# Threshold attention in front of a routed expert layer: the attention rewritten as a five-step pipeline with a written order on every engine

## The chip, the cores and the metric

The kernel runs on one core of one Trainium2 chip. The time is the device time of one execution in microseconds (us); the median of three runs stands for the kernel. A core has five engines that run their own instruction streams and wait for each other through semaphores: TensorE (PE, with its weight loads as PEld), VectorE (DVE), ScalarE (ACT), GpSimd (POOL) and SyncE (SP, which here issues DMAs). TensorE writes to PSUM only; POOL can't reach PSUM.

## The reference

Attention over 8 batches, 8 heads, 576 rows and 64 columns, with a threshold below the row's maximum, then a two-layer expert network whose expert follows from the token's id:

```python
scores = (1 / sqrt(64)) * (q @ k.transpose(0, 1, 3, 2))          # (8, 8, 576, 576)
thresh = scores.max(-1, keepdims=True) - tau
scores = where(scores >= thresh, scores, -1e9)
attn = exp(scores - scores.max(-1, keepdims=True))
attn = attn / (attn.sum(-1, keepdims=True) + 1e-09)
x = (attn @ v).transpose(0, 2, 1, 3).reshape(4608, 512)
expert = token_ids * 2654435761 % 8
for e in range(8):
    out[expert == e] = maximum(x[expert == e] @ w1[e], 0) @ w2[e]  # 512 -> 1024 -> 512
```

All of it is fp32.

## The kernel before

Two heads are worked on together, a pair `p`; there are 32 of them. k and q come in transposed, the 64 columns of one head on partitions 0 to 63 and those of the other on 64 to 127, so that the score matmuls of the two heads use the two row halves of TensorE's array. A pair has nine score tiles of 128 rows and 576 columns: four for each head (units 0 to 7) and one (unit 8) that holds the last 64 rows of both heads. A tile takes two PSUM banks, and `ps_sc` has room for two tiles.

`score` (L135) issues the matmuls of two tiles and calls `weigh` (L156) for each: the row maximum from PSUM on DVE (L160), two operations on one column each that make the exponent's bias and the threshold (L161, L163), the exponential from PSUM on ACT (L167), and on DVE the mask (L169): it compares the scores, read from PSUM a second time, with the threshold, multiplies with the exponentials and sums the row. `turn_head` and `turn_tail` (L174, L188) transpose the masked weights `w` of a pair in pieces of 128 by 128, four to a PSUM bank, and ACT copies each bank to `wT` in SBUF (L186, L194, L199). `av_half` (L202) multiplies them with v, 288 columns at a time, the two heads in the two column halves of the array. `put_x` (L218) copies the result to `oT`, transposes it back, scales it by the row sums (DVE, L243, L247) into a tile for the whole batch, and after every fourth pair `store_x` (L253) writes the batch to `x_scratch` in HBM from POOL's queue.

`route` (L262) builds the table that tells which tokens each expert gets. It is called once, after the second pair's scores. The main loop (L422 on) writes out the order of TensorE's instructions by hand: in round `p` the five groups of scores of pair `p` alternate with the transposes, AV and output of pair `p - 1`. The order on the other engines is the scheduler's. The experts' part (L448 on) follows: it gathers rows of x by the table (POOL), transposes them, and runs two chains of matmuls for each expert (L479, L493).

## Time and profile before

| | before |
|---|---|
| time, median of 3 runs | 1472.01 us (1471.65 to 1475.71) |
| profiled execution: time, span | 1471.82 us, 1470.2 us |
| busy share of the span: PE, PEld, DVE, ACT, POOL | 85%, 51%, 43%, 33%, 8% |
| mean granted TensorE clock | 0.955 |
| DMA, mean over the span | 62 GB/s |
| chain of work that ended last | "issue" 8%, DMA 2%: it is only followed through the last stores |

The shares are means over two parts with different limits: up to about 880 us DVE and ACT work all the time and PE has gaps; behind that PE is full and the others are nearly idle. So the profile is read by stretches of time, and within attention by the waits of each engine. The page's chain that ended last covers the last 147 us alone and says nothing about attention.

### The profile page before, as it was taken

What the parts mean: (1) busy time and instruction counts of PE and PEld (TensorE: products, weight loads), DVE (VectorE), ACT (ScalarE), POOL (GpSimd) and SP (SyncE); (2) the same over time, 40 slices, a digit from 0 to 9 for tenths busy, and PEclk for the clock granted to TensorE, in tenths of its full rate; (3) what the DMA queues carried; (4) which work ended last, traced back from release to release, by engine and by line L of the source; (5) the groups of instructions that cost most, each with busy time, mean ns of one, the idle gap of its engine ahead of it and who ended that gap; (6) DMA issues with size and microseconds to landing.
All of it is one profiled execution on the core that took longest, in us unless ns stands there. A gap on an engine that the chain in (4) does not pass through costs nothing. (4 is left out here: it accounts for less than half of the span.)

```text
span 1470.2 us, 15795 instructions
## 1 busy us (share of the span) xinstructions
PE 1249.7 (85%) x5894; PEld 746.4 (51%) x5894; DVE 633.1 (43%) x1773; ACT 483.9 (33%) x809; POOL 111.7 (8%) x127
## 2 busy tenths in 40 slices
PE   4568777878878787887878777999999999999997
PEld 2344445544544554445544445565656564646463
DVE  5756676666666666676666651101000101001000
ACT  2334545455454554545455540000000000000000
POOL 0030000000000000000000004101010202010101
PEclk9878999999899999999899998999999999999999
DMA  8200210210201102012001003223232313121000
GB/s 304 70 8 26 81 33 17 88 26 23 91 17 56 58 24 91 17 33 81 25 26 49 1 18 114 95 85 107 74 108 69 110 69 118 62 86 59 32 1 33
DMA packets 41198, 91.27 MB, mean 62 GB/s; under 512 B 9116, under 2 KB 9116, under 8 KB 41120
## 3 DMA queue, kind: packets, MB, share of 16 engines
q1 hardware_dynamic: 32032, 61.91, 13.0%
q0 software_dynamic: 9088, 28.32, 5.7%
q8 instruction: 48, 0.79, 0.2%
q14 instruction: 30, 0.25, 0.1%
HBM read 72.39 MB, written 19.92 MB: 63 GB/s over the span
## 5 line engine op out<-in xcount | busy, mean ns | idle before, releaser
L151 PE MATMUL sc<-k_sb,q 64*128 64x288 f32 (+1 forms) x1152 | 259.4, 460 | 88.5 <-DVE w L169 69.3
L167 ACT ACTIVATE w<-sc,bia,scl 128x576 f32<-128x576 f32 x288 | 225.9, 830 | 194.6 <-DVE bia L161 194.5
L184 PE MATMUL tr<-ident,w 128*128 128x128 f32 (+1 forms) x1280 | 209.7, 312 | 86.0 <-ACT wT L186 84.3
L160 DVE TENSOR_REDUCE mx<-sc 128x1 f32<-128x576 f32 x288 | 207.1, 753 | 174.5 <-PE sc L151 174.3
L493 PE MATMUL o_ps<-w_sb,h_sb 128*128 128x512 f32 x640 | 280.6, 592 | 0.0
L479 PE MATMUL h_ps<-xT,w_sb 128*128 128x320 f32 x1024 | 277.5, 433 | 0.0
L169 DVE SCALAR_TENSOR_TENSOR w<-sc,thr,w 128x576 f32<-128x576 f32 x288 | 225.3, 816 | 102.4 <-ACT w L167 101.4
L186 ACT COPY wT<-tr 128x512 f32<-128x512 f32 (+1 forms) x320 | 176.6, 591 | 193.1 <-PE tr L184 192.9
L479 PEld LDWEIGHTS h_ps<-xT,w_sb 128*128 128x128 f32 x1024 | 194.9, 190 | 83.4 <-issue 3.7
L151 PEld LDWEIGHTS sc<-k_sb,q 64*128 64x128 f32 (+1 forms) x1152 | 138.7, 198 | 184.1 <-issue 121.2
L184 PEld LDWEIGHTS tr<-ident,w 128*128 128x128 f32 (+1 forms) x1280 | 154.0, 151 | 152.5 <-ACT wT L186 117.8
L493 PEld LDWEIGHTS o_ps<-w_sb,h_sb 128*128 128x128 f32 x640 | 118.9, 190 | 136.0 <-issue 135.8
L213 PE MATMUL av<-wT,v_sb 128*64 128x288 f32 (+1 forms) x1280 | 178.7, 415 | 0.0
L487 DVE TENSOR_SCALAR h_sb<-h_ps 128x640 f32<-128x640 f32 x32 | 26.4, 825 | 298.9 <-PE h_ps L479 288.4
L213 PEld LDWEIGHTS av<-wT,v_sb 128*64 128x64 f32 (+1 forms) x1280 | 80.3, 135 | 84.6 <-issue 46.5
L496 ACT COPY o_sb<-o_ps 128x512 f32<-128x512 f32 x40 | 23.4, 586 | 300.5 <-PE o_ps L493 300.5
L472 DVE COPY xT<-xT_ps 128x512 f32<-128x512 f32 x40 | 27.6, 690 | 193.3 <-PE xT_ps L471 192.3
L485 ACT ACTIVATE h_sb<-h_ps 128x640 f32<-128x640 f32 x32 | 22.5, 704 | 239.3 <-PE h_ps L479 239.3
L260 POOL DMA_DIRECT2D x_scratch<-xt x16 | 9.9, 619 | 776.6 <-DVE xt L247 776.6
L463 POOL DMA_INDIRECT xg<-x_scratch,gidx x40 | 40.6, 1016 | 273.4 <-PE xT_ps L471 264.0
L161 DVE TENSOR_SCALAR bia<-mx,nscl 128x1 f32<-128x1 f32 x288 | 58.7, 204 | 0.0
L163 DVE TENSOR_SCALAR thr<-mx,drop 128x1 f32<-128x1 f32 x288 | 58.7, 204 | 0.0
(92 smaller groups left out, 380.6 us busy)
## 6 DMA issues: line engine op xcount, KB each, us to landing
w_sb<-in_moe_w_dram SPq DMA_DIRECT2D x16, 2048.0 KB, 8.8
k_sb<-in_k_dram SPq DMA_DIRECT2D x32, 288.0 KB, 2.9
q<-in_q_dram SPq DMA_DIRECT2D x32, 256.0 KB, 2.7
v_sb<-in_v_dram SPq DMA_DIRECT2D x8, 1024.0 KB, 5.4
x_scratch<-xm POOLq DMA_DIRECT2D x8, 1024.0 KB
q<-in_q_dram SPq DMA_DIRECT2D x64, 16.0 KB, 2.6
v_sb<-in_v_dram SPq DMA_DIRECT2D x8, 128.0 KB, 4.0
x_scratch<-xt POOLq DMA_DIRECT2D x16, 64.0 KB
```

The costliest lines, as they stand in the source:

```text
L151: nc.tensor.matmul(scs[u][:, i, 0:S2], lhsT=q_sb[rows, cols], rhs=k_sb[rows, S2 * i:S2 * i + S2], start=True, stop=True)
L160: nc.vector.tensor_reduce(out=mx[:], in_=sc[:, :, 0:S2], axis=AX.XY, op=ALU.max)
L161: nc.vector.tensor_scalar(out=bia[:], in0=mx[:], scalar1=nscl[:], scalar2=None, op0=ALU.mult)
L163: nc.vector.tensor_scalar(out=thr[:], in0=mx[:], scalar1=drop[:], scalar2=None, op0=ALU.subtract)
L167: nc.scalar.activation(w3, sc[:, :, 0:S2], AF.Exp, bias=bia[:], scale=scl[:])
L169: nc.vector.scalar_tensor_tensor(out=w3, in0=sc[:, :, 0:S2], scalar=thr[:], in1=w3, op0=ALU.is_ge, op1=ALU.mult, accum_out=rs[:, u:u + 1])
L184: nc.tensor.transpose(tr[0:kn, P * t:P * t + P], ws[4 * j + t][:, k0:k0 + kn], ident[:])
L186: nc.scalar.copy(wT[0:kn, c, j, 0:TAIL], tr[0:kn, :])
L213: nc.tensor.matmul(av[64 * j:64 * j + 64, i, 0:S2], lhsT=v_sb[0:kn, c, h * D:h * D + D], rhs=wT[0:kn, c, j, S2 * i:S2 * i + S2], start=(c ...
L463: nc.gpsimd.indirect_dma_start(out=xg[:], out_offset=None, in_=x_dram[:, :], in_offset=bass.IndirectOffsetOnAxis(ap=idx, axis=0), bounds_c ...
L479: nc.tensor.matmul(h_ps[:, i, 0:width], lhsT=w1_sb[:, co, fo * P:fo * P + P], rhs=xT[:, co, i * width:i * width + width], start=(co == 0), ...
L493: nc.tensor.matmul(o_ps[:], lhsT=h_sb[:, fo, kt * P:kt * P + P], rhs=w2_sb[:, fo, :], start=(fo == 0), stop=(fo == FO - 1))
```

## The change

Attention becomes a pipeline over 160 steps `n`, five for each pair (`p, s = divmod(n, 5)`; in step s = 0 the tile with the last rows of both heads, in s = 1 to 4 one tile of each head). In step `n` the engines do:

- scores of step `n + 1` (PE), into the same two PSUM tiles;
- `negate` of step `n` (DVE): one operation copies a tile from PSUM to SBUF as `ns`, with the sign changed, and gives the row minimum of that; POOL adds the threshold (`thr`); ACT takes the exponential from `ns`;
- `mask` of step `n - 1` (DVE), from `ns` and `w`, both in SBUF;
- `turn_w` and `put_wT` of step `n - 2`: transposes by halves of 64 rows into the two banks of one PSUM tile, and one copy of 640 columns by ACT;
- AV of the pair before, in four parts over s = 1 to 4 (320 columns in s = 1 and 2, 256 in s = 3 and 4), `put_oT` behind each half;
- in s = 0 the output of the pair two back: `turn_o` writes its transposes into the PSUM tile of AV, `put_x` scales them (one DVE operation, two on ACT) and SP stores x for that pair.

The factor 1/8 and the case of a negative tau go into q (`scale_q`, on POOL). v is loaded per pair. The last chunk of `w` and v is filled up with zeros to 128. `route` is a generator, one piece of which is issued behind each step from `n = 7` on. The order is written out for all engines, not for TensorE alone. The ten zeroed buffers of the expert part are set up by POOL at the start instead of by DVE behind attention; the first experts' weights are loaded from pair 20 on instead of pair 4.

TensorE's order for one pair. Before, from the third score group of a pair to the next pair's first; `sc` are scores, `tr` with `w` turned weights, `tr` with `oT` the output turned back:

```order
L151 MATMUL sc<-k_sb,q_117 128x288 x4
L184 MATMUL tr<-ident,w 128x128 x16
L184 MATMUL tr<-ident,w 64x128 x4
L151 MATMUL sc<-k_sb,q_117 128x288 x4
L193 MATMUL tr<-ident,w 128x128 x4
L198 MATMUL tr<-ident,w 64x128
L213 MATMUL av<-wT,v_sb 64x288 x10
L151 MATMUL sc<-k_sb,q_117 128x288 x4
L213 MATMUL av<-wT,v_sb 64x288 x10
L151 MATMUL sc<-k_sb,q_117 128x288 x2
L238 MATMUL tr<-ident,oT 128x128 x4
```

Now, from step s = 1 of a pair to its step s = 4:

```order
L241 MATMUL av<-wT_a,v_121 64x320 x4
L215 MATMUL tr<-ident,w_124 128x64 x10
L168 MATMUL sc<-k_sb,q_119 128x288 x4
L215 MATMUL tr<-ident,w_125 128x64 x10
L241 MATMUL av<-wT_a,v_121 64x320 x6
L215 MATMUL tr<-ident,w_126 128x64 x10
L168 MATMUL sc<-k_sb,q_119 128x288 x4
L241 MATMUL av<-wT_b,v_121 64x256 x6
L215 MATMUL tr<-ident,w_127 128x64 x10
L168 MATMUL sc<-k_sb,q_119 128x288 x4
L215 MATMUL tr<-ident,w_128 128x64 x10
```

AV stands in four parts of two or three chunks instead of two of five, and a turned tile is ten short transposes in one row instead of a share of sixteen and four.

DVE's order, before, two groups of scores:

```order
L160 TENSOR_REDUCE mx<-sc 128x1 x2
L161 TENSOR_SCALAR bia<-mx,nscl 128x1
L163 TENSOR_SCALAR thr<-mx,drop 128x1
L161 TENSOR_SCALAR bia<-mx,nscl 128x1
L163 TENSOR_SCALAR thr<-mx,drop 128x1
L169 SCALAR_TENSOR_TENSOR w,rs<-sc,thr,w 128x576 x2
L160 TENSOR_REDUCE mx<-sc 128x1 x2
```

Now, from step s = 3 to the output scaling in the next pair's s = 0:

```order
L180 TENSOR_SCALAR ns,nmx<-sc 128x576 x2
L204 SCALAR_TENSOR_TENSOR w_126,rs<-ns,thr,w_126 128x576
L204 SCALAR_TENSOR_TENSOR w_127,rs<-ns,thr,w_127 128x576
L180 TENSOR_SCALAR ns,nmx<-sc 128x576 x2
L204 SCALAR_TENSOR_TENSOR w_128,rs<-ns,thr,w_128 128x576
L204 SCALAR_TENSOR_TENSOR w_129,rs<-ns,thr,w_129 128x576
L180 TENSOR_SCALAR ns,nmx<-sc 128x576
L204 SCALAR_TENSOR_TENSOR w_123,rs<-ns,thr,w_123 128x576
L204 SCALAR_TENSOR_TENSOR w_124,rs<-ns,thr,w_124 128x576
L256 TENSOR_SCALAR rec<-rs 128x9
L258 RECIPROCAL rec<-rec 128x9
```

The first two-tile operation of a step frees the scores' PSUM tiles, and the masks that follow are those of the step before.

The diff, cut to its core (of the lines taken out, most of which are printed above, only some stand here):

```diff
+    WA, WB = 64 + 2 * P, 2 * P
...
+         tc.tile_pool(name="a_ns", bufs=5) as a_ns, \
...
-         tc.tile_pool(name="ps_tr", bufs=2, space=PSUM) as ps_tr, \
+         tc.tile_pool(name="ps_tr", bufs=1, space=PSUM) as ps_tr, \
...
+        v_bufs = [a_q.tile([P, NC, P], FP32, name=f"v_{i}") for i in range(3)]
+        NW = 7
+        w_bufs = [a_q.tile([P, NC * P], FP32, name=f"w_{i}") for i in range(NW)]
+        wT = [a_q.tile([P, 2, NC, WA], FP32, name="wT_a"),
+              a_q.tile([P, 2, NC, WB], FP32, name="wT_b")]
+        oT = a_o.tile([P, 64 + S], FP32, name="oT")
+        av = ps_av.tile([P, 2, 512], FP32, name="av")
...
+            for j in range(2):
+                nc.sync.dma_start(out=q_sb[64 * j:64 * j + 64, TAIL + 64 * j:TAIL + 64 * j + 64],
+                                  in_=qT[b, h0 + j, :, TAIL:S])
             nc.sync.dma_start(out=k_sb[:], in_=kT[b, h0:h0 + 2].rearrange("h d s -> (h d) s"))
...
+        def load_v(p):
+            b, hp = divmod(p, HP)
+            v_sb = v_bufs[p % 3]
+            rows = v[b].rearrange("s h d -> s (h d)")[:, hp * P:hp * P + P]
+            nc.sync.dma_start(out=v_sb[:, 0:4],
+                              in_=rows[0:TAIL].rearrange("(c p) m -> p c m", p=P))
+            nc.sync.dma_start(out=v_sb[0:64, 4], in_=rows[TAIL:S])
+        def scale_q(p):
+            q_sb = q_bufs[p % 3]
+            nc.gpsimd.tensor_scalar(out=q_sb[:], in0=q_sb[:], scalar1=keep_any[:], scalar2=SCALE,
+                                    op0=ALU.mult, op1=ALU.mult)
+        def heads(n):
+            return 1 if n % NS == 0 else 2
+        def score(n):
+            p, s = divmod(n, NS)
             q_sb, k_sb = q_bufs[p % 3], kts[p]
-            scs = {}
-            for u in us:
-                sc_new = ps_sc.tile([P, 2, 512], FP32, name="sc")
-                scs[u] = sc_new
+            for j in range(heads(n)):
+                sc = ps_sc.tile([P, 2, 512], FP32, name="sc")
+                scs[n, j] = sc
             for i in range(2):
-                for u in us:
...
+                for j in range(heads(n)):
+                    if s == 0:
+                        rows, cols = slice(0, P), slice(TAIL, TAIL + P)
                     else:
-                        rows, cols = slice(0, P), slice(TAIL, TAIL + P)
-                    nc.tensor.matmul(scs[u][:, i, 0:S2], lhsT=q_sb[rows, cols],
+                        rows, cols = slice(64 * j, 64 * j + 64), slice(P * (s - 1), P * s)
+                    nc.tensor.matmul(scs[n, j][:, i, 0:S2], lhsT=q_sb[rows, cols],
...
-                weigh(p, u, scs[u])
...
-            w = a_w.tile([P, S], FP32, name="w")
-            w3 = w[:].rearrange("p (i s) -> p i s", i=2)
-            nc.scalar.activation(w3, sc[:, :, 0:S2], AF.Exp, bias=bia[:], scale=scl[:])
-            rs = pend[p]["rs"]
-            nc.vector.scalar_tensor_tensor(out=w3, in0=sc[:, :, 0:S2], scalar=thr[:], in1=w3,
-                                           op0=ALU.is_ge, op1=ALU.mult,
-                                           accum_out=rs[:, u:u + 1])
-            pend[p]["w"][u] = w
...
-                    nc.tensor.transpose(tr[0:kn, P * t:P * t + P],
-                                        ws[4 * j + t][:, k0:k0 + kn], ident[:])
-                nc.scalar.copy(wT[0:kn, c, j, 0:TAIL], tr[0:kn, :])
...
+        def negate(n):
+            nmx = a_st.tile([P, 2], FP32, name="nmx")
...
+            stats[n] = (nmx, thr)
+            for j in range(heads(n)):
+                sc = scs.pop((n, j))
+                ns = a_ns.tile([P, S], FP32, name="ns")
+                nss[n, j] = ns
+                nc.vector.tensor_scalar(out=ns[:].rearrange("p (i s) -> p i s", i=2),
+                                        in0=sc[:, :, 0:S2], scalar1=-1.0, scalar2=None,
+                                        op0=ALU.mult, op1=ALU.min, accum_out=nmx[:, j:j + 1])
+            nj = heads(n)
+            nc.gpsimd.tensor_scalar(out=thr[:, 0:nj], in0=nmx[:, 0:nj], scalar1=drop[:],
+                                    scalar2=None, op0=ALU.add)
+        def expo(n, j):
+            w = w_bufs[w_count[0] % NW]
...
+            ws[n, j] = w
+            nc.scalar.activation(w[:, 0:S], nss[n, j][:], AF.Exp, bias=stats[n][0][:, j:j + 1],
+                                 scale=-1.0)
...
+        def mask(n, j):
...
+            u = 8 if s == 0 else 2 * (s - 1) + j
+            w = ws[n, j]
+            nc.vector.scalar_tensor_tensor(out=w[:, 0:S], in0=nss.pop((n, j))[:],
+                                           scalar=stats[n][1][:, j:j + 1], in1=w[:, 0:S],
+                                           op0=ALU.is_le, op1=ALU.mult,
+                                           accum_out=rss[p][:, u:u + 1])
+        def turn(dst, src, cols):
+            for c, (lo, hi) in enumerate(cols):
+                for r, c0 in ((0, lo), (1, hi)):
+                    rows = slice(64 * r, 64 * r + 64)
+                    nc.tensor.transpose(dst[:, r, 64 * c:64 * c + 64], src[rows, c0:c0 + P],
+                                        ident[rows, rows])
+        KCOLS = [(P * c, P * c) for c in range(NC)]
+        def turn_w(n, j):
+            tr = ps_tr.tile([P, 2, 512], FP32, name="tr")
+            turn(tr, ws.pop((n, j)), KCOLS)
+            return tr
+        def put_wT(n, j, tr):
+            s = n % NS
+            src = tr[:, :, 0:64 * NC].rearrange("p r (c q) -> p r c q", c=NC)
+            if s == 0:
+                dst = wT[0][:, :, :, 0:64]
+            else:
+                c0 = 64 + P * (s - 1) if s < 3 else P * (s - 3)
+                dst = wT[s // 3][:, j, :, c0:c0 + P].rearrange("p c (r q) -> p r c q", r=2)
+            nc.scalar.copy(dst, src)
+        def av_part(p, g, chunks):
+            width = (WA, WB)[g]
+            for c in chunks:
+                for j in range(2):
+                    nc.tensor.matmul(av[64 * j:64 * j + 64, g, 0:width],
+                                     lhsT=v_bufs[p % 3][:, c, 64 * j:64 * j + 64],
+                                     rhs=wT[g][:, j, c, :], start=(c == 0), stop=(c == NC - 1))
+        def put_oT(g):
+            c0, width = ((64, WA), (64 + WA, WB))[g]
+            nc.scalar.copy(oT[:, c0:c0 + width], av[:, g, 0:width])
+        def turn_o():
+            turn(av, oT, [(P * (t + 1), P * (t + 1)) for t in range(NQ)] + [(64, 0)])
...
-            nc.vector.tensor_scalar(out=rec[:], in0=rs[:], scalar1=1e-9, scalar2=None,
+            nc.vector.tensor_scalar(out=rec[:], in0=rss.pop(p)[:], scalar1=1e-9, scalar2=None,
                                     op0=ALU.add)
             nc.vector.reciprocal(rec[:], rec[:])
...
-                nc.tensor.transpose(om[:, P * t:P * t + P], oT[:, P * t:P * t + P], ident[:])
-            ot = ps_tr.tile([P, 512], FP32, name="tr")
-            nc.tensor.transpose(ot[:, 0:P], oT[:, TAIL:TAIL + P], ident[:])
-            om4 = om[:].rearrange("p (t m) -> p t m", t=NQ)
+            xm = a_x.tile([P, NQ, P], FP32, name="xm")
+            xt = a_x.tile([P, D], FP32, name="xt")
...
+                nc.scalar.mul(xt[half, :], av[half, j, 4 * D:5 * D], rec[half, 8:9])
+            r0, c0 = b * S, hp * P
+            nc.sync.dma_start(
+                out=x_dram[r0:r0 + TAIL, c0:c0 + P].rearrange("(t p) m -> p t m", p=P), in_=xm[:])
             for j in range(2):
-                nc.gpsimd.dma_start(out=tail[j], in_=xt[64 * j:64 * j + 64])
+                nc.sync.dma_start(out=x_dram[r0 + TAIL:r0 + S, c0 + D * j:c0 + D * j + D],
+                                  in_=xt[64 * j:64 * j + 64, :])
...
+            yield
...
+                yield
+                yield
+                tr = ps_tr.tile([P, 2, 512], FP32, name="tr")
+                inv = tr[:, 0, 0:2 * NHI]
...
-            acc = rt_sb.tile([P, 2 * NHI], FP32, name="acc")
...
+                if c0 == 0:
+                    nc.vector.tensor_copy(acc[:], inv)
+                else:
+                    nc.vector.tensor_tensor(out=acc[:], in0=acc[:], in1=inv, op=ALU.add)
+                yield
...
+        scale_q(0)
...
+        for w in w_bufs:
+            nc.vector.memset(w[:, S:NC * P], 0.0)
...
-        with tc.manual_schedule(engines={mybir.EngineType.PE}):
-            for p in range(NP + 1):
...
+        LAST = NS * NP
+        pieces = route()
+        with tc.manual_schedule():
+            for xg in xg_bufs:
+                nc.gpsimd.memset(xg[:], 0.0)
+            score(0)
+            for n in range(LAST + NS + 1):
+                p, s = divmod(n, NS)
+                m = n - 2
+                if s == 0 and p + 2 < NP:
...
+                if s == 0 and p + 1 < NP:
+                    load_v(p + 1)
+                if s == 1 and p + 1 < NP:
+                    scale_q(p + 1)
+                if s == 2 and p in (20, 24):
+                    load_w1(p // 4 - 5)
+                if s == 2 and p in (22, 26):
+                    load_w2((p - 22) // 4)
+                done = p - 1
+                av_ok = 0 <= done < NP
+                if av_ok and s in (1, 2):
+                    av_part(done, 0, ((0, 1), (2, 3, 4))[s - 1])
+                if av_ok and s in (3, 4):
+                    av_part(done, 1, ((0, 1, 2), (3, 4))[s - 3])
+                back = p - 2 if s == 0 else -1
+                if back >= 0:
+                    turn_o()
+                turned = 0 <= m < LAST
+                if turned:
+                    tr = turn_w(m, 0)
+                if n < LAST:
+                    negate(n)
+                    expo(n, 0)
+                if turned:
+                    put_wT(m, 0, tr)
+                if n < LAST and heads(n) == 2:
+                    expo(n, 1)
+                if n + 1 < LAST:
+                    score(n + 1)
+                if 0 < n <= LAST:
+                    for j in range(heads(n - 1)):
+                        mask(n - 1, j)
+                if av_ok and s in (2, 4):
+                    put_oT(s // 2 - 1)
+                if turned and heads(m) == 2:
+                    tr = turn_w(m, 1)
+                    put_wT(m, 1, tr)
+                if back >= 0:
+                    put_x(back)
+                if n >= NS + 2:
+                    next(pieces, None)
...
-        xg_bufs = [m_xg.tile([P, DIN], FP32, name=f"xg_{i}") for i in range(2 * KT)]
-        for xg in xg_bufs:
-            nc.vector.memset(xg[:], 0.0)
```

## Rows read from the trace of the kernel before

**Rows 1.** Busy time by stretch: PE, PEld, DVE, ACT, POOL (count), PE clock, DMA share, GB/s

```profile
62.20:91.50 29.30, 7.05 (x45) 5.48 (x46) 20.40 (x42) 0.00 (x0) 13.01 (x8) 0.53 0.00 1
91.50:878.80 787.30, 634.80 (x3862) 385.74 (x3862) 519.75 (x1537) 415.96 (x704) 14.11 (x22) 0.95 0.13 41
878.80:895.70 16.90, 5.16 (x21) 3.81 (x22) 6.42 (x12) 0.00 (x0) 9.64 (x11) 0.53 0.53 160
895.70:1470.20 574.50, 566.35 (x1805) 329.93 (x1804) 50.62 (x68) 45.98 (x72) 72.91 (x73) 1.00 0.22 75
```

**Rows 2.** Waits between 300 and 860 us: total us, times, longest us

```profile
ACT w L167 <- DVE bia L161: 124.3, 65, 3.5
DVE mx L160 <- PE sc L151: 114.5, 111, 3.0
```

**Rows 3.** Instructions in time order, one step: start us, us, engine, line [idle before]

```profile
508.86 1.24 PE L151 MATMUL sc<-k_sb,q 64*128 64x288 f32 x8
...
510.13 1.42 DVE L160 TENSOR_REDUCE mx<-sc 128x1 f32<-128x576 f32 x2 [1.48 <-PE sc L151]
510.72 1.07 ACT L186 COPY wT<-tr 128x512 f32<-128x512 f32 x2 [1.18 <-PE tr L184]
...
511.71 1.55 ACT L167 ACTIVATE w<-sc,bia,scl 128x576 f32<-128x576 f32 x2
...
512.57 0.82 DVE L169 SCALAR_TENSOR_TENSOR w<-sc,thr,w 128x576 f32<-128x576 f32 x1 [0.53 <-ACT w L167]
513.15 1.07 ACT L186 COPY wT<-tr 128x512 f32<-128x512 f32 x2
...
513.31 0.81 DVE L169 SCALAR_TENSOR_TENSOR w<-sc,thr,w 128x576 f32<-128x576 f32 x1
...
514.34 1.24 PE L151 MATMUL sc<-k_sb,q 64*128 64x288 f32 x8
```

**Rows 4.** Timeline of ACT: first and last of 14 successive copies of `av`

```profile
523.75 0.64 ACT L224 COPY oT<-av 128x576 f32<-128x576 f32 x1
...
859.83 0.64 ACT L224 COPY oT<-av 128x576 f32<-128x576 f32 x1
```

**Rows 5.** Timeline of PE and PEld in short windows; a row merges like instructions

```profile
509.20 0.65 PE L151 MATMUL sc<-k_sb,q 64*128 64x288 f32 x4
...
510.03 0.20 PEld L184 LDWEIGHTS tr<-ident,w 128*128 128x128 f32 x2 [0.39 <-issue]
510.03 0.33 PE L184 MATMUL tr<-ident,w 128*128 128x128 f32 x1
510.03 0.55 PE L184 MATMUL tr<-ident,w 128*128 128x128 f32 x3
510.08 0.25 PEld L184 LDWEIGHTS tr<-ident,w 128*128 128x128 f32 x2
...
520.57 0.40 PE L151 MATMUL sc<-k_sb,q 64*128 64x288 f32 x1
520.90 0.14 PEld L213 LDWEIGHTS av<-wT,v_sb 128*64 128x64 f32 x2 [0.39 <-issue]
```

**Rows 6.** Timeline of SP: two DMA issues in a row

```profile
525.62 1.11 SPq L125 DMA_DIRECT2D q<-in_q_dram  x2
```

**Rows 7.** Groups and tile `hi` in 60 to 92 us: ns mean, or min/median/max

```profile
L310 DVE TENSOR_TENSOR cs<-incl,cs 128x288 f32<-128x288 f32 x1 | 0.5, 458 | 0.0
L381 DVE SCALAR_TENSOR_TENSOR val<-acc 128x72 f32<-128x72 f32 x1 | 0.2, 232 | 0.0
...
L369 POOL TENSOR_TENSOR hi<-hi,parts_h x8: 1262/1502/2307, 72.7 to 86.8; 128x648 f16<-128x648 f16 x8
L364 DVE TENSOR_TENSOR hi<-iota_h,parts_h x4: 821/1358/1896, 71.8 to 82.5; 128x648 f16<-128x648 f16 x4
```

**Rows 8.** Busy time by stretch, as rows 1, around a fall of the clock

```profile
530.50:533.90 3.40, 3.40 (x16) 2.97 (x16) 1.26 (x6) 1.91 (x4) 0.00 (x0) 0.50 0.01 2
533.90:551.00 17.10, 14.46 (x97) 8.06 (x96) 11.48 (x33) 10.58 (x18) 0.00 (x0) 0.97 0.05 15
```

More of the change, by code (lines that the diff above doesn't have):

```diff
@@ L49 @@
     TAIL = NQ * P
-    KC = [(c * P, min(P, S - c * P)) for c in range(5)]
+    NC = 5
+    NS = 5
+    WA, WB = 64 + 2 * P, 2 * P
     KT = 5
@@ L78 @@
     drop = consts.tile([P, 1], FP32, name="drop")
-    scl = consts.tile([P, 1], FP32, name="scl")
-    nscl = consts.tile([P, 1], FP32, name="nscl")
     gidx = consts.tile([P, NHI], I32, name="gidx")
     ov_i = consts.tile([P, NOV + 1], I32, name="ov_i")
+    xg_bufs = [consts.tile([P, DIN], FP32, name=f"xg_{i}") for i in range(2 * KT)]
     w_tiles = {}
@@ L123, in load_pair @@
                               in_=qT[b, h0:h0 + 2, :, 0:TAIL].rearrange("h d s -> (h d) s"))
-            for j in range(2):
-                nc.sync.dma_start(out=q_sb[64 * j:64 * j + 64, TAIL + 64 * j:TAIL + 64 * j + 64],
-                                  in_=qT[b, h0 + j, :, TAIL:S])
-            if hp == 0:
-                v_sb = a_v.tile([P, 5, H * D], FP32, name="v_sb")
-                vts[b] = v_sb
-                rows = v[b].rearrange("s h d -> s (h d)")
-                nc.sync.dma_start(out=v_sb[:, 0:4],
-                                  in_=rows[0:TAIL].rearrange("(c p) m -> p c m", p=P))
-                nc.sync.dma_start(out=v_sb[0:64, 4], in_=rows[TAIL:S])
@@ L135, in score @@
-        def score(p, us):
+        def load_v(p):
[9 more added lines that the diff above has]
+                                    op0=ALU.mult, op1=ALU.mult)
@@ L202, in av_half @@
[L202 to L216 removed]
+        def negate(n):
+            nmx = a_st.tile([P, 2], FP32, name="nmx")
+            thr = a_st.tile([P, 2], FP32, name="thr")
+            stats[n] = (nmx, thr)
[9 more added lines that the diff above has]
+                                    scalar2=None, op0=ALU.add)
@@ L234, in put_x @@
-            xm, xt = xs[b]
-            c0 = 2 * hp * D
-            om = ps_tr.tile([P, 512], FP32, name="tr")
-            for t in range(NQ):
-                nc.tensor.transpose(om[:, P * t:P * t + P], oT[:, P * t:P * t + P], ident[:])
-            ot = ps_tr.tile([P, 512], FP32, name="tr")
-            nc.tensor.transpose(ot[:, 0:P], oT[:, TAIL:TAIL + P], ident[:])
-            om4 = om[:].rearrange("p (t m) -> p t m", t=NQ)
+            xm = a_x.tile([P, NQ, P], FP32, name="xm")
+            xt = a_x.tile([P, D], FP32, name="xt")
@@ L355, in route @@
             nc.vector.tensor_copy(parts_h[:], parts[:])
-            inv = ps_tr.tile([P, 512], FP32, name="tr")
+            yield
+            acc = rt_sb.tile([P, 2 * NHI], FP32, name="acc")
+            val = rt_sb.tile([P, NHI], FP32, name="val")
+            emp = rt_sb.tile([P, NHI], FP32, name="emp")
             M = 9
@@ L450 @@
+    with tc.tile_pool(name="m_x", bufs=2) as m_x, \
          tc.tile_pool(name="m_h", bufs=2) as m_h, \
```

159 lines of the change are left out of this document (39 added, 120 removed).

## The prediction

> **What bounds the kernel now.** I read the busy time by stretch first [rows 1]. From the first score to the last store of x the kernel is in attention (5.8 to 878.8 us, the table-building `route()` in between at 62.2 to 91.5), then 16.9 us pass until the first expert matmul, and then TensorE is busy 566.35 of 574.50 us. The expert part is at TensorE's limit and the change leaves its instructions alone; all that can move is the 873.0 us of attention. There no engine is full: over 787.3 us PE is busy 634.8, DVE 519.8, ACT 416.0. So a chain of waits bounds it, and the table of waits says which [rows 2]: ACT waits for DVE's `bia`, DVE for the scores. The order of one step shows the rest [rows 3]: scores from 508.86, row maxima from 510.13, exponentials from 511.71, masks from 512.57 to 514.1, and at 514.34 the next scores, since a score's PSUM tile is held until its mask has read it. One step of two score tiles takes 5.48 us, while its scores fill 1.24 us of PE. The copy of `av` comes once per head pair; from the 1st to the 14th shown it took (859.83 - 523.75) / 13 = **25.85 us per pair** [rows 4]. 32 pairs are 827.2; with `route()`'s 29.3, in which attention stands still [rows 1], 16.5 of the 873.0 are left for the first and the last round.
>
> **What the change removes.** The score tile is now free after one DVE pass (`negate`: copy to SBUF, negated, with the row minimum). So the loop that holds scores back shrinks to scores, two negates, scores. The two one-column operations per tile go away (`bia` is no longer needed, `thr` goes to POOL). And the masks, exponentials and transposes of a step belong to earlier steps, so none waits for work just begun. What is left is the sum on each engine in each of the five steps of a pair. I work that out.
>
> **TensorE.** Scores: the two row halves run at the same time, and four passes, two by two, end 0.65 us after they start, where the last alone takes 0.40 [rows 5]; so a pass of 288 columns on both halves costs 0.245. Four of them and a first load of 0.1 make 1.07 a step, the single tile the same. AV has the same two passes, so a 128-row chunk of 320 columns is 2 x 0.27 = 0.54, one of 256 columns 0.43. A change between the array's shapes costs: from the last score (520.57) to the next shape's load is 0.33 (520.90), 0.09 more than the pass, and I add 0.05 for the slower first one: 0.14 each, at the start and end of each AV part, and around the one score tile that uses all 128 rows. Transposes: now one of 128 columns each, spaced (0.55 - 0.33) / 2 = 0.11 with 0.33 for the first alone; loads of 128 columns follow each other 0.05 to 0.06 apart (510.03 and 510.08). The new form has 64 streaming columns, so half of 0.11, and loads of 128 columns; twice as many, but alternating between row halves, which in the score rows run together. **Price of one turned tile:** if pass, load and both halves overlap, 5 x 0.057 + 0.06 = 0.35; if load and pass of a half don't overlap, 5 x 0.112 + 0.06 = 0.62; if the halves don't overlap either, 1.18. Before it was 5 x 0.11 = 0.55. I take 0.35, because both overlaps are in the score rows: two passes at once, and passes of 288 columns that leave no room between them for a load.
>
> Per step s of a pair (AV chunks; tiles turned), PE has: s0 three tiles turned (one is the output) and a score, 2.1; s1 1.08 + 0.28 + 0.70 + 1.07 = 3.1; s2 1.62 + 0.28 + 0.35 + 1.07 = 3.3; s3 1.29 + 0.28 + 0.70 + 1.07 = 3.3; s4 0.86 + 0.56 + 0.70 + 1.07 = 3.2.
>
> **VectorE.** A mask starts 0.74 after the one before (512.57, 513.31), accumulator read included [rows 3]. I take the same for a negate, which also streams 576 columns from PSUM and reads the accumulator. Steps s2 to s4 have two of each, 2.96; s1 2.2; s0 one negate, two masks and the output scaling (about 1.0 for three operations), 3.2, and AV of s1 waits for the end of that scaling, since it rewrites the same PSUM tile. **ScalarE:** two exponentials hold it from 511.71 to 513.15, 0.72 each; two copies of 512 columns from 510.72 to 511.71, 0.50 each [rows 3], so 0.62 for 640 columns: 2.7 a step, 3.0 with a copy of `av`. It is nowhere the longest.
>
> **Sum.** Longest engine of each step: 3.2 + 3.1 + 3.3 + 3.3 + 3.2 = 16.1. The engines hand over to each other within a step (two turns behind one PSUM tile, each waiting for ACT's copy; scores behind negates), which the totals hide; I add 0.25 a step, about five handovers of 0.05 as between 508.86 + 1.24 and 510.13: 16.1 + 1.25 = 17.4, taken as **17.5 us per pair**, 25.85 - 17.5 = 8.35 less, over 32 pairs **-267**. `route()` is cut into pieces behind the steps: its 20.4 us on DVE [rows 1] ran alone, now DVE has some 3 us free in a pair, so of about five pairs 13 to 15 are hidden, and POOL's products delay a few thresholds; I leave 9 of 29.3: **-20**. Start: POOL scales q before the first score (nearest row of that width, 1.26 [rows 7]), and its ten memsets stand before the first threshold: **+3**. First and last round as before; the 16.9 us into the experts stay, as SP's small last stores take the place of POOL's. SP issues nine DMAs a pair instead of about five (v per pair, x per pair); at 1.11 for two [rows 6] that is 5 us of 17.5, and no engine needs one that is younger than a step, so 0; were SP late, scores would wait. Profiled execution 1471.8 (span 1470.2 and 1.6 around it; the median of the runs, 1472.0, is the same within 0.2) - 267 - 20 + 3 = 1188. **Forecast 1190**, its own range 1150 (no handover time, 16.2 a pair) to 1220 (18.4).
>
> **A page against a row.** In before, each mask had one input in PSUM; now both are fp32 in SBUF. The nearest rows with two such inputs run at full rate: from 72 to 288 columns 458 - 232 = 226 ns more for 216 columns [rows 7], 1.05 ns a column; but neither reads the accumulator. The Trainium skill (Vector Engine (DVE) Microarchitecture Reference, Points that are easy to get wrong) states that this very operation with two non-bf16 SBUF sources halves its throughput. By the rows the mask stays at 0.74; the other result is rival 2.
>
> **Rivals.**
> 1. *Halves don't overlap.* For: no row shows a transpose by row halves. At 0.62 a tile, seven turns in s1 to s4 add 0.27 each, s0 stays below DVE: 19.4 a pair, 1190 + 61 = **1250**. With the halves one after the other, 1.18: seven times 0.83 and s0 at 4.6 make 24.7, 32 x 1.15 = 37 less than before: 1472 - 37 - 20 + 3 = **1418**.
> 2. *The mask at half rate.* At 2.1 ns a column it is 0.74 + 0.60 = 1.34. DVE becomes the longest: s0 4.4, s2 to s4 4.16 each, s1 3.1 by PE: 20.0, with handovers 20.4; and DVE no longer hides `route()`: 1472 - 174 - 9 + 3 = **1292**. Against: the two rows of 72 columns.
> 3. *POOL and DVE block each other.* With POOL's products beside it DVE's `hi` took up to 1896 ns instead of 821, and POOL's own up to 2307 instead of 1262 [rows 7]. Now POOL works in every step. Price of the scaling of q from 0.3 to 1.26, of a threshold 0.1 to 0.3: at most 0.36 in s1, where DVE has 0.9 to spare, and a threshold has a whole step's time. 0.5 a pair: **1205**, inside the forecast's range.
> 4. *Slower: the TensorE clock.* It falls after idle time: over 530.5 to 533.9 it is granted 0.50, the 1.2 GHz level, and in the whole stretch 0.95 [rows 1, 8]. At 1.2 GHz throughout, every pass doubles: s0 4.1, s1 5.9, s2 6.3, s3 6.3, s4 5.6, with handovers 29.4 a pair, 32 x 3.55 = 114 more: 1472 + 114 - 20 + 3 = **1569**. It ends slower from 26.4 a pair on, a mean clock of about 0.57. Against: before's gaps of about 2 us at the end of a pair fill up. In 530.5 to 533.9 PE had transposes only (16, all the time), and right behind it the clock is 0.97. The Trainium skill (TensorE: Matmul & The Clock Gate, Part 4) says that transposes don't count as PE work in the same way; by that rule more transpose time would speak for this rival, but the row shows the clock back up after nothing but transposes.
> 5. *The pipeline doesn't pipeline*: a wait that I don't see keeps the chain at 25 us a pair: about **1470**. Against: the waits in the new order name only work of an earlier step, but for score and negate.
>
> **Chances.** Forecast with rival 3: 0.57. Rival 1 at 1250: 0.18, at 1418: 0.06. Rival 2: 0.13. Rival 4: 0.04. Rival 5: 0.02. The range takes in the forecast, 1250 and 1292 (0.88): 1150 to 1295. About 0.3% can be told from no change: faster 0.94, same 0.02, slower 0.04.
>
> **What would show it.** Right: the copies of `av` come 16 to 18.5 us apart per pair; a turned tile's ten transposes start within 0.4 us; negate and mask start 0.74 apart; PE waits mostly for DVE's scaling in s0; clock near 1.0; 570 to 580 us from the first expert matmul. Rival 1: ten transposes over 0.6 or 1.1 us and PE without idle time. Rival 2: masks of 1.4 us, DVE full. Rival 3: masks of mixed length next to POOL's work. Wrong altogether: a granted clock of 0.5, or waits of more than 1 us in each step.

## The result and the profile after

| | before | after |
|---|---|---|
| time, median of four runs each | 1471.83 us (1471.06 to 1475.71) | **1199.28 us** (1198.08 to 1200.82) |
| ratio to before, 95% interval | | 0.8144 (0.8127 to 0.8162) |
| span of the profiled execution | 1470.2 us | 1199.2 us |
| PE, DVE, ACT, POOL busy | 85%, 43%, 33%, 8% | 90%, 44%, 40%, 21% |
| granted TensorE clock | 0.955 | 0.980 |

Forecast were 1190 us, with 1150 to 1220 as its own range. So the size was met; the question is whether it was met for the reasons given.

Busy time by stretch of the changed kernel, columns as in [rows 1]: most of the pairs with pieces of `route()`, the steady pairs, the last round, the gap, the experts.

```profile
33.90:139.60 105.70, 89.84 (x928) 56.68 (x930) 90.48 (x240) 68.38 (x112) 38.07 (x38) 0.94 0.20 57
139.60:583.00 443.40, 380.71 (x4406) 237.46 (x4400) 353.81 (x981) 340.42 (x551) 120.73 (x150) 1.00 0.27 84
583.00:607.10 24.10, 16.21 (x160) 8.84 (x156) 7.39 (x22) 9.66 (x18) 1.14 (x2) 0.79 0.07 21
607.10:619.50 12.40, 5.29 (x21) 3.77 (x22) 2.77 (x4) 0.00 (x0) 7.95 (x8) 0.55 0.46 132
619.50:1199.20 579.70, 567.07 (x1805) 330.36 (x1804) 50.64 (x68) 45.98 (x72) 73.19 (x73) 0.99 0.22 74
```

The copy of AV's second half comes once per pair, as the copy in [rows 4] did. The timeline of ACT shows these two, 18 pairs apart:

```profile
233.44 0.36 ACT L247 COPY oT<-av 128x256 f32<-128x256 f32 x1
...
552.58 0.36 ACT L247 COPY oT<-av 128x256 f32<-128x256 f32 x1
```

(552.58 - 233.44) / 18 = **17.73 us per pair**, where [rows 4] gave 25.85. The six pairs that carry `route()`, from one negate of step s = 0 (24.12) to that six pairs on (144.97), are longer, together 14.5 us more than six of 17.73. The span divides as follows:

| | before | after | difference |
|---|---|---|---|
| up to the first score | 5.8 | 7.7 | +1.9 |
| 32 pairs | 827.2 | 567.4 | -259.8 |
| `route()` beyond its cover | 29.3 | 14.5 | -14.8 |
| first and last round | 16.5 | 17.5 | +1.0 |
| last store of x to first expert matmul | 16.9 | 12.4 | -4.5 |
| first expert matmul to the end | 574.5 | 579.7 | +5.2 |
| sum | 1470.2 | 1199.2 | -271.0 |

What is waited for now, between 200 and 500 us (17 pairs), in the view of [rows 2]:

```profile
DVE ns L180 <- PE sc L168: 56.7, 51, 1.8
...
PE av L241 <- ACT xt L268: 23.5, 17, 1.4
...
PE av L241 <- ACT oT L247: 13.7, 17, 0.8
```

ACT's wait for `bia`, 124.3 us in [rows 2], is gone, and DVE's wait for scores is now mostly the echo of two waits of TensorE: once per pair 1.4 us for `xt` (the scaled last rows of the two heads) and once 0.8 us for `oT`, both written by ACT. One pair in order of time, in the view of [rows 3], from the negate of step s = 2 to that of the next s = 2:

```profile
400.19 0.76 DVE L180 TENSOR_SCALAR_CACHE_REDUCE ns<-sc 128x576 f32<-128x576 f32 x1 [1.79 <-PE sc L168]
400.88 0.75 DVE L180 TENSOR_SCALAR_CACHE_REDUCE ns<-sc 128x576 f32<-128x576 f32 x1
401.55 0.81 DVE L204 SCALAR_TENSOR_TENSOR w<-ns,thr,w 128x576 f32<-128x576 f32 x1
401.80 0.72 POOL L184 TENSOR_SCALAR thr<-nmx,drop 128x2 f32<-128x2 f32 x1 [3.25 <-DVE ns L180]
402.29 0.81 DVE L204 SCALAR_TENSOR_TENSOR w<-ns,thr,w 128x576 f32<-128x576 f32 x1
402.56 1.19 PE L168 MATMUL sc<-k_sb,q 64*128 64x288 f32 x8
403.41 0.78 ACT L191 ACTIVATE w<-ns,nmx 128x576 f32<-128x576 f32 x1
403.78 0.76 DVE L180 TENSOR_SCALAR_CACHE_REDUCE ns<-sc 128x576 f32<-128x576 f32 x1 [0.67 <-PE sc L168]
404.08 0.42 ACT L247 COPY oT<-av 128x320 f32<-128x320 f32 x1
404.55 1.52 PE L241 MATMUL av<-wT_b,v 128*64 128x256 f32 x12 [0.80 <-ACT oT L247]
...
407.58 0.76 DVE L180 TENSOR_SCALAR_CACHE_REDUCE ns<-sc 128x576 f32<-128x576 f32 x1 [0.88 <-PE sc L168]
410.57 0.76 DVE L180 TENSOR_SCALAR_CACHE_REDUCE ns<-sc 128x576 f32<-128x576 f32 x1
412.21 1.28 POOL L148 TENSOR_SCALAR q<-q,keep_any 128x640 f32<-128x640 f32 x1
413.35 0.69 DVE L261 TENSOR_TENSOR xm<-av,rec 128x512 f32<-128x512 f32 x1 [0.20 <-DVE rec L258]
413.82 0.69 ACT L233 COPY wT_b<-tr 128x640 f32<-128x640 f32 x1 [0.68 <-PE tr L215]
413.96 0.75 DVE L180 TENSOR_SCALAR_CACHE_REDUCE ns<-sc 128x576 f32<-128x576 f32 x1
414.41 0.64 ACT L268 ACTIVATE xt<-av,rec 64x64 f32<-64x64 f32 x2
415.11 1.30 PE L241 MATMUL av<-wT_a,v 128*64 128x320 f32 x8 [1.38 <-ACT xt L268]
416.33 0.39 PEld L215 LDWEIGHTS tr<-ident,w 64*128 64x128 f32 x10 [0.49 <-issue]
416.64 0.79 PEld L168 LDWEIGHTS sc<-k_sb,q 64*128 64x128 f32 x8
417.93 0.76 DVE L180 TENSOR_SCALAR_CACHE_REDUCE ns<-sc 128x576 f32<-128x576 f32 x1 [1.79 <-PE sc L168]
```

The reader sees three things. A turned tile takes TensorE 0.31 us (416.33 to 416.64). A negate follows the other after 0.69, a mask starts 0.74 after the one before. And in front of both AV rows TensorE has stood still for a copy that ACT made late: `oT` at 404.08 behind an exponential, `xt` at 414.41 behind the second copy of a turned tile.

### The profile page after: what moved, and what is told of

Read it like the earlier page. It is cut to its first block, busy times and chain, and to the rows that moved or that the text cites. A ratio compares the mean times of both kernels' runs of the same rounds, so it can differ in the third digit from the quotient of the medians.

```text
span 1199.2 us, 19456 instructions
## 1 busy us (share of the span) xinstructions
PE 1082.9 (90%) x7494; PEld 652.3 (54%) x7494; DVE 527.9 (44%) x1390; ACT 482.4 (40%) x777; POOL 256.1 (21%) x305
## 5 line engine op out<-in xcount | busy, mean ns | idle before, releaser
L180 DVE TENSOR_SCALAR_CACHE_REDUCE ns<-sc 128x576 f32<-128x576 f32 x288 | 207.7, 754 | 98.8 <-PE sc L168 97.3
L191 ACT ACTIVATE w<-ns,nmx 128x576 f32<-128x576 f32 x288 | 224.0, 778 | 34.9 <-DVE ns L180 32.0
L204 DVE SCALAR_TENSOR_TENSOR w<-ns,thr,w 128x576 f32<-128x576 f32 x288 | 228.1, 826 | 0.0
L184 POOL TENSOR_SCALAR thr<-nmx,drop 128x2 f32<-128x2 f32 (+1 forms) x160 | 117.9, 737 | 400.0 <-DVE ns L180 400.0
L215 PEld LDWEIGHTS tr<-ident,w 64*128 64x128 f32 x2880 | 115.9, 140 | 108.6 <-ACT wT_a L233 43.0
L215 PE MATMUL tr<-ident,w 64*128 64x64 f32 x2880 | 153.5, 233 | 9.3 <-ACT wT_a L233 6.5
L545 DVE TENSOR_SCALAR h_sb<-h_ps 128x640 f32<-128x640 f32 x32 | 26.4, 825 | 299.6 <-PE h_ps L537 299.6
L554 ACT COPY o_sb<-o_ps 128x512 f32<-128x512 f32 x40 | 23.4, 586 | 300.5 <-PE o_ps L551 300.5
L241 PE MATMUL av<-wT_a,v 128*64 128x320 f32 x640 | 105.2, 460 | 41.7 <-ACT xt L268 41.7
L233 ACT COPY wT_a<-tr 128x640 f32<-128x640 f32 x160 | 110.7, 692 | 65.9 <-PE tr L215 63.3
L233 ACT COPY wT_b<-tr 128x640 f32<-128x640 f32 x128 | 88.5, 691 | 60.3 <-PE tr L215 60.1
L241 PE MATMUL av<-wT_b,v 128*64 128x256 f32 x640 | 83.2, 390 | 24.9 <-ACT oT L247 24.7
```

What stands on the lines that cost most here:

```text
L180: nc.vector.tensor_scalar(out=ns[:].rearrange("p (i s) -> p i s", i=2), in0=sc[:, :, 0:S2], scalar1=-1.0, scalar2=None, op0=ALU.mult, op1= ...
L184: nc.gpsimd.tensor_scalar(out=thr[:, 0:nj], in0=nmx[:, 0:nj], scalar1=drop[:], scalar2=None, op0=ALU.add)
L191: nc.scalar.activation(w[:, 0:S], nss[n, j][:], AF.Exp, bias=stats[n][0][:, j:j + 1], scale=-1.0)
L204: nc.vector.scalar_tensor_tensor(out=w[:, 0:S], in0=nss.pop((n, j))[:], scalar=stats[n][1][:, j:j + 1], in1=w[:, 0:S], op0=ALU.is_le, op1= ...
L215: nc.tensor.transpose(dst[:, r, 64 * c:64 * c + 64], src[rows, c0:c0 + P], ident[rows, rows])
L233: nc.scalar.copy(dst, src)
```

## Experiments

The reasons under test: theory A, the gain came from the short hold of the score tile and from what it lets a written order do, and what is left is TensorE's own work with two waits behind ACT's queue; rivals, that the written order alone did it, that VectorE sets the time, that turning by halves counts for little. Each ratio below is to the kernel before on the same chip, with its 95% interval.

**The negate alone, in the kernel before** (`e9_negate_alone`). Edit in `weigh`:

```diff
-            nc.vector.tensor_reduce(out=mx[:], in_=sc[:, :, 0:S2], axis=AX.XY, op=ALU.max)
+            nc.vector.tensor_scalar(out=ns3, in0=sc[:, :, 0:S2], scalar1=-1.0, scalar2=None,
+                                    op0=ALU.mult, op1=ALU.min, accum_out=nmx[:])
...
-            nc.scalar.activation(w3, sc[:, :, 0:S2], AF.Exp, bias=bia[:], scale=scl[:])
+            nc.scalar.activation(w3, ns3, AF.Exp, bias=bia[:], scale=nscl[:])
```

> One part of the change alone, in the kernel before: the row maximum becomes the copy to SBUF with sign and row minimum, and the exponential and the mask read that copy. TensorE's order, the scheduler's order on the other engines, the full transposes, AV, x and route() stay as they were (one buffer instead of two in route() for room). VectorE's order still has both masks of a step ahead of the next step's copies, so copies 1.4, bias 0.2, two exponentials 1.5 and the last mask 0.75 stay in one chain, but the scores, 1.24 and a hand-over of 0.25, lie beside it. Theory A (the short hold is the larger part of the gain): 4.0 a step where 5.48 was, about 21 us a pair instead of 25.85, about 1317 us. Rival B (without the order written for all engines the copies of turned tiles on ScalarE stay in the chain): 24 to 25 a pair, 1410 us or more.

Measured 1339.18 us, 0.9092 (0.9073 to 0.9110). The copies of `av` in ACT's timeline, 18 pairs apart:

```profile
294.92 0.62 ACT L228 COPY oT<-av 128x576 f32<-128x576 f32 x1
...
683.69 0.62 ACT L228 COPY oT<-av 128x576 f32<-128x576 f32 x1
```

That is 21.6 a pair: theory A's 21, and not rival B's 24 to 25. The time is 22 us above its 1317, of which the 0.6 a pair make 19. VectorE did not get less to do by it. Busy time over 13 pairs of the kernel before and over 18 of this one, columns as in [rows 1]:

```profile
523.75:859.83 336.08, 270.84 (x1638) 164.78 (x1638) 224.22 (x664) 177.30 (x301) 5.88 (x9) 0.94 0.12 37
```

```profile
294.92:683.69 388.77, 343.31 (x2269) 208.31 (x2269) 309.02 (x1081) 250.93 (x416) 9.80 (x15) 0.98 0.18 55
```

That is 17.2 us of VectorE a pair in both, so it is the hold that went, and not work. One edit, in `weigh` alone, carries about half of the whole gain. The other half, 140 us, is not taken apart to its end: in the changed kernel the turning by halves is worth 72 us and `route()` in pieces 21.7, as below, and the rest (the order on all engines, AV in four parts, the thresholds on POOL) has no run of its own with the short hold.

**Everything but the negate** (`e2_hold_scores`, `e7_hold_reordered`). The exponential and the mask read PSUM again, and the mask stands in the step of its scores:

```diff
-            nc.scalar.activation(w[:, 0:S], nss[n, j][:], AF.Exp, bias=stats[n][0][:, j:j + 1],
-                                 scale=-1.0)
+            nc.scalar.activation(w[:, 0:S].rearrange("p (i s) -> p i s", i=2),
+                                 scs[n, j][:, :, 0:S2], AF.Exp, bias=stats[n][0][:, j:j + 1],
+                                 scale=1.0)
...
+                if n < LAST:
+                    for j in range(heads(n)):
+                        mask(n, j)
                 if n + 1 < LAST:
                     score(n + 1)
-                if 0 < n <= LAST:
-                    for j in range(heads(n - 1)):
-                        mask(n - 1, j)
```

> One part undone: the exponential and the mask read the scores from PSUM again, and the mask stands in the step of its scores, so that a score tile is held until its mask has read it. The copy to SBUF still runs (its result is written and not used), the transposes, AV, x and the written order stay. Theory A (the gain came from the short hold of the score tile): a step is scores 1.2, first negate 0.7, second 0.7 beside the first exponential, second exponential behind a copy of the turned tile (ends about 4.3), second mask 0.75: 5.1 us; four of these and 3.7 for the single tile: 24.1 a pair instead of 17.73, +204: about 1400 us. Rival B (the gain came from the order written out for all engines and from turning tiles two steps later): below 1290 us.

Measured 1667.34 us, 1.1313 (1.1283 to 1.1343): far above both numbers. In its trace the second turned tile stood in TensorE's order behind scores that waited for a mask, ACT's copy of it behind that, and the next exponential behind the copy:

```profile
415.23 1.80 PE L168 MATMUL sc<-k_sb,q 64*128 64x288 f32 x5 [1.66 <-DVE w L206]
...
416.84 1.21 PE L217 MATMUL tr<-ident,w 64*128 64x64 f32 x7
...
418.14 0.69 ACT L235 COPY wT_b<-tr 128x640 f32<-128x640 f32 x1 [3.82 <-PE tr L217]
...
418.73 0.75 ACT L191 ACTIVATE w<-sc,nmx 128x576 f32<-128x576 f32 x1
```

The second kernel moves `score(n + 1)` behind the second turned tile:

```diff
                 if turned and heads(m) == 2:
                     tr = turn_w(m, 1)
                     put_wT(m, 1, tr)
+                if n + 1 < LAST:
+                    score(n + 1)
```

> Scores held in PSUM until their mask, as in the run that took 1667 us, but TensorE turns both tiles of a step ahead of the next scores. In that run the second turned tile stood behind scores that waited for a mask, ScalarE's copy of it behind that, and the next exponential behind the copy. Theory A (the held tile costs a step of about 5.1 us, the rest was this queue): 4 x 5.1 + 3.6 = 24 us a pair, 32 x 6.3 more than the changed kernel: about 1400 us, and at most 1470 where the clock falls in the gaps. Rival B (the order has little to do with it): above 1600 us.

Measured 1571.70 us, 1.0695 (1.0622 to 1.0769): between the two, and still slower than before. Busy time between 200 and 500 us, columns as in [rows 1], and one step of its trace:

```profile
200.00:500.00 300.00, 230.70 (x1815) 129.17 (x1815) 155.87 (x407) 137.62 (x225) 21.20 (x61) 0.82 0.14 40
```

```profile
407.70 0.76 DVE L180 TENSOR_SCALAR_CACHE_REDUCE ns<-sc 128x576 f32<-128x576 f32 x1 [0.86 <-PE sc L168]
408.50 0.74 ACT L191 ACTIVATE w<-sc,nmx 128x576 f32<-128x576 f32 x1 [1.79 <-DVE ns L180]
...
410.45 0.69 ACT L235 COPY wT_a<-tr 128x640 f32<-128x640 f32 x1 [1.21 <-PE tr L217]
411.04 0.75 ACT L191 ACTIVATE w<-sc,nmx 128x576 f32<-128x576 f32 x1
411.82 0.82 DVE L206 SCALAR_TENSOR_TENSOR w<-sc,thr,w 128x576 f32<-128x576 f32 x1 [1.39 <-ACT w L191]
412.79 1.21 PE L168 MATMUL sc<-k_sb,q 64*128 64x288 f32 x6 [1.49 <-DVE w L206]
413.58 0.76 DVE L180 TENSOR_SCALAR_CACHE_REDUCE ns<-sc 128x576 f32<-128x576 f32 x1 [0.94 <-PE sc L168]
```

The step is 5.88 us here, at a granted clock of 1.00 (407.0 to 413.6); of the 0.78 above the expected 5.1, most is the second exponential, which waits from 409.2 to 411.0 for its turn behind the copy of a tile that TensorE turned behind AV. But the pairs are not all alike. Two of them, from copy to copy of `av`'s second half, columns as in [rows 1]:

```profile
307.78:334.16 26.38, 19.25 (x176) 11.05 (x176) 14.96 (x39) 13.49 (x24) 2.10 (x6) 0.92 0.16 47
365.00:395.84 30.84, 24.58 (x183) 13.59 (x181) 15.14 (x39) 13.48 (x23) 2.09 (x6) 0.74 0.13 38
```

At a clock of 0.92 a pair takes 26.4 us, 0.5 more than before, where the clock was 0.94; at 0.74 it takes 30.8. So most of the 100 us above the kernel before come with the fallen clock: over the whole stretch, with TensorE idle a quarter of the time, its mean is 0.82. In the same 300 us VectorE's masks also waited 19.1 us for POOL's threshold, a handover that the kernel before does not have. So the written order is no gain by itself: with held scores it is no faster than the scheduler's at about the same clock, and slower in all. It is the rival "the written order did it" that falls; theory A's size for the hold was too small, 8.7 us a pair (26.4 - 17.73) where it had 6.3, and it did not have the clock. An order written for a long hold was not tried.

**Full transposes** (`e1_full_turn`):

```diff
-            turn(tr, ws.pop((n, j)), KCOLS)
+            flat, w = tr[:].rearrange("p r m -> p (r m)"), ws.pop((n, j))
+            for c in range(NC):
+                nc.tensor.transpose(flat[:, P * c:P * c + P], w[:, P * c:P * c + P], ident[:])
```

> The weights are turned by five full transposes of 128 x 128 per tile, as in the kernel before, instead of ten by row halves; nothing else changes. Theory A (TensorE's own order of work is the chain: in the changed kernel it stands still only 2.5 us of a pair's 17.73): a turned tile goes from 0.36 to 5 x 0.11 = 0.55 us, nine tiles a pair, 1.7 us a pair, 32 pairs: +55, about 1254 us. Rival B (VectorE or the hand-overs set the step, TensorE has room for 1.7 us of its idle 2.5): at most +10, about 1205 us. If full transposes cost more than 0.11 next to the row-half scores (a change of shape at 0.14 each side, as between scores and AV): up to +2.5 more a pair, 1330 us.

Measured 1271.57 us, 0.8638 (0.8621 to 0.8656), 72 more than the changed kernel; a pair takes 20.39. A turned tile and the scores behind it, timeline of PE and PEld:

```profile
503.78 0.53 PEld L224 LDWEIGHTS tr<-ident,w 128*128 128x128 f32 x5 [0.49 <-issue]
503.78 0.76 PE L224 MATMUL tr<-ident,w 128*128 128x128 f32 x5
504.47 0.79 PEld L168 LDWEIGHTS sc<-k_sb,q 64*128 64x128 f32 x8 [0.17 <-issue]
```

0.69 instead of 0.31. That fits 5 x 0.11 and 0.14 for the change of shape to the row halves of the scores, which the last sentence of the expectation had allowed for. Rival B, that TensorE has room, falls: nine tiles by 0.38 are 3.4, and 2.66 of them reach the pair.

**Where what is left is lost** (`e4_x_early`, `e5_oT_early`, `e6_both_early`). Only the order changes: in s = 0 `put_x` moves up, and `put_oT` moves behind the first exponential.

```diff
+                if back >= 0:
+                    make_rec(back)
                 if n < LAST:
                     negate(n)
                     expo(n, 0)
+                if av_ok and s in (2, 4):
+                    put_oT(s // 2 - 1)
                 if turned:
                     put_wT(m, 0, tr)
+                if back >= 0:
+                    put_x(back)
```

> In step s = 0 the scaling of the output moves ahead: VectorE makes the reciprocals before the negate and xm before the two masks, ScalarE scales xt behind the first copy of a turned tile instead of behind the second. Theory A: AV of s = 1 now waits 1.4 us per pair for xt, and would then start when TensorE is through with the second turned tile; no other engine is late there: -1.3 a pair over 30 pairs, -40, about 1160 us. Rival B: VectorE's masks, now 0.7 later, or the next hand-over take its place: -10 or less, 1190 us or more.

> The copy of a finished half of AV to oT moves ahead on ScalarE: behind the step's first exponential instead of behind its second. Theory A: in the changed kernel TensorE stands still 0.80 us a pair in front of AV's second half until that copy is done (it only frees the AV tile; the copy's own time is 0.4), and the copy waits in ScalarE's order behind an exponential that waits for nothing TensorE does: -0.75 a pair, 31 pairs, -23, about 1176 us. Rival B: AV's second half goes into the other bank and waits for something else that ends at the same time: 0, about 1199 us.

> The two moves together: output scaling early (-35.6 us when done alone) and oT early. Theory A (the waits stand one behind the other in TensorE's order and add): 16.50 us a pair go to about 15.6, close to the 15.3 us that TensorE is busy in a pair; about 1138 us. Rival B (VectorE, busy 85% of the time when the output scaling is early, becomes the one that is waited for): 1155 us or more.

Measured: `x` early 1163.67 us, 0.7902 (0.7887 to 0.7916); `oT` early 1175.85, 0.7975 (0.7959 to 0.7992); both 1139.53, 0.7738 (0.7720 to 0.7756). Pairs take 16.50, 16.88 and 15.64. All three are theory A's numbers within 4 us, and the gains add (35.6 + 23.4 = 59.0; measured 59.8). Busy time of the kernel with both, columns as in [rows 1]:

```profile
200.00:500.00 300.00, 288.73 (x3380) 188.20 (x3380) 275.93 (x752) 261.41 (x424) 76.03 (x116) 1.00 0.35 105
```

TensorE is now busy 96% of these 300 us and VectorE 92%: this is where moves of this kind end.

**route()** (`e3_route_whole`, `e10_route_spread`). Once in one go, once in the kernel with both moves with one piece per pair:

```diff
-                if n >= NS + 2:
+                if n >= NS + 2 and s == 2:
                     next(pieces, None)
```

> route() is issued in one go behind step 7 instead of one piece behind each step; attention and experts are unchanged. In the changed kernel the six pairs with pieces of it take 14.5 us more than six pairs of 17.73. In the kernel before the whole took 29.3. Theory A (the pieces hide half of it): +15, about 1214 us. Rival B (VectorE's 20 us for it are paid either way, and the order in pieces brings nothing): +0 to +5, about 1202 us.

> The kernel with both moves (1139.5 us), and route()'s pieces one per pair, behind the masks of step s = 2, instead of one per step from step 7. In that kernel the six pairs with pieces took 21 us more than six pairs of 15.63, though VectorE then waits for scores some 0.8 us a pair at that place. Theory A: a piece is 20.4 / 27 = 0.76 us on VectorE and fits into that wait: some 15 of the 21 us vanish, about 1124 us. Rival B: VectorE is busy 92% of the time, so each piece pushes what follows: 1139 us as before.

Measured 1220.97 us, 0.8285 (0.8271 to 0.8299), 21.7 more: the pair that holds the whole of it takes 53.16, that is 35.4 beyond 17.73, where pieces cost 14.5. So the pieces hide more than theory A's 15. And 1126.46 us, 0.7650 (0.7632 to 0.7668), for the spread form, 13.1 less than with both moves: a piece of some 0.76 us fits where VectorE waits for scores, but not into every step. This is the fastest kernel of the study.

**The stores of x** (`e8_x_by_batch`):

```diff
-            nc.sync.dma_start(
-                out=x_dram[r0:r0 + TAIL, c0:c0 + P].rearrange("(t p) m -> p t m", p=P), in_=xm[:])
+            if hp < HP - 1:
+                return
...
+            nc.gpsimd.dma_start(out=x_dram[r0:r0 + TAIL].rearrange("(t p) m -> p t m", p=P),
+                                in_=xm[:])
```

> x is gathered into one tile per batch of four pairs again and stored from POOL's queue behind the fourth, as in the kernel before; the rest is the changed kernel. Theory A: the stores per pair lie beside the work and cost nothing (pairs stay at 17.73), but the last store is four times as large and leaves from the queue that gathers x: the gap from the last store's issue to the first expert matmul, 12.4 us in the changed kernel, goes back towards 16.9: +4, about 1203 us. Rival B: SyncE's nine issues a pair or their transfers do hold something up: pairs shorter by 0.2 or more, 1193 us or less.

Measured 1197.96 us, 0.8130 (0.8113 to 0.8146): not to be told from the changed kernel. Pairs stay at 17.73, as theory A had it, and the gap grows by 1.8 to 14.2 us, less than its 4. What pays this back stands at the end of the chain that ended last, here of the changed kernel and of this one (start us, us):

```profile
1187.79 0.70 POOL out_dram L555
```

```profile
1186.52 0.71 POOL out_dram L561
```

Behind this last issue the changed kernel's span goes on for 1199.2 - 1188.5 = 10.7 us, this one's for 1193.6 - 1187.2 = 6.4, the kernel before's for 6.2. That is 4.5 of the 5.2 us which the last row of the table above showed.

## Why the prediction held, and where it did not

**The bound.** Right: the chain through a held score tile. Taken away alone it gives 134 us, put back into the changed kernel it costs over 370, the fall of the clock included.

**Price of one turned tile.** 0.35 was taken, 0.31 measured. Both overlaps read from the score rows hold for transposes, so rival 1 is out at both its prices. The halves are worth 72 us, more than a term of 7 x 0.2 a pair would give, because the full form also pays a change of shape that the sum had priced only around AV and the one score tile of 128 rows.

**VectorE.** Negate 0.69 (0.74 was taken), mask 0.74, as taken. Rival 2 is out: the mask reads two fp32 sources in SBUF and reads the accumulator, and 402.29 - 401.55 = 0.74 is what it took from PSUM [rows 3]. The Trainium skill's sentence (Vector Engine (DVE) Microarchitecture Reference, Points that are easy to get wrong) that this operation then halves its throughput is not borne out here. Rival 2's own price was too low: it added 0.4 for handovers where the forecast added 1.25. With 1.25 its pair is 21.2 and its time about 1319, outside the stated 1295.

**The sum.** 17.5 a pair against 17.73, but its steps are less good than its total:

| step | s0 | s1 | s2 | s3 | s4 |
|---|---|---|---|---|---|
| predicted, with 0.25 | 3.45 | 3.35 | 3.55 | 3.55 | 3.45 |
| measured, negate to negate | 3.39 | 3.97 | 3.59 | 3.80 | 2.99 |

TensorE's own sum was right (15.0; it is busy 257.6 of 300 us, 15.2 a pair). **The step that failed is the allowance for handovers**: five of 0.05 a step, spread evenly. (The row that the 0.05 was read from shows 0.03.) In truth hardly anything is lost at most handovers, and 2.2 us at two places. The prediction said that AV of s = 1 waits for the end of the scaling, but followed it on VectorE, where it ends at 414.04, and not into ACT's queue, where `xt` ends at 415.05; `oT` in front of AV's second half it did not follow at all. "ScalarE is nowhere the longest" was true of its sum and misleading about its order. The surplus of s1 and s3 (0.62 + 0.25) meets s4, which came out 0.46 shorter: there TensorE has no late copy in front of it. That the total came out within 0.23 us is in part luck: two waits that the sum did not follow stood against an allowance for others that hardly exist. The experiments with `xt` and `oT` show that these two waits were nearly the whole of the difference to TensorE's own time (17.73 to 15.64, of which it is busy 15.05).

**route().** 9 us were to remain, 14.5 did: six pairs, not five, carried it, and in the 105.70 us that hold most of the pieces VectorE was busy 90.48, so that pieces came faster than its gaps. The run with one piece per pair shows that the cover was there, at another pace.

**Smaller terms.** The start cost 1.9 instead of 3. The gap in front of the experts was to stay and fell by 4.5; the end was to stay and grew by 5.2. These two nearly cancel, which is luck, and the prediction had neither.

**Rivals 3 to 5.** Rival 3 is there in mechanism and costs the changed kernel nothing that its trace shows, as below. Rival 4 is out: the clock is 1.00 over the steady pairs, with twice as many transposes as before in less time, and also 1.00 between 200 and 500 us with the full transposes, which take longer. It shows in the kernels with held scores: 0.82, with TensorE idle a quarter of the time. Rival 5 is out.

## What to carry to other kernels

When a PSUM tile is held through a chain of engines, first look for one pass that takes all later readers off it; only then write an order for the engines: here an order written for a short hold gained nothing over the scheduler's with a long one. Sum the engines per step, but then follow each small copy at the seams through the queue of the engine that makes it: an engine that is 77% busy can still hold the fullest one up twice per round. Work without a due time goes into the gaps at the pace of the gaps, not one piece per step.
